# Splitting the first weight load of a decode block: 4,096 columns by themselves, as 112 plain rows and 8 groups of 2 rows

## The chip, the cores and the metric

The kernel runs on one core of a Trainium2 chip. The metric is the device time of one execution in microseconds. The time before is 374.37 us, the median of three runs (374.28 to 374.49). A profile is one execution recorded by the hardware profiler; its times count from the start of its span.

## The reference

One step of decoding for a batch of two, in float32: a layer norm, grouped-query attention over a cache of 4,096 positions, and a bilinear gated branch that scales the attention's output.

```python
def _A_ref(x, k_cache, v_cache, wq, wo):          # Hq 16, Hkv 8, Sk 4096, Dh 256, D 448
    q = (x @ wq).reshape(B, Sq, Hq, Dh) ...
    k = jnp.repeat(k_cache, rep, axis=1)
    v = jnp.repeat(v_cache, rep, axis=1)
    scores = jnp.einsum("bhqd,bhkd->bhqk", q, k) * (Dh ** -0.5)
    p = _softmax(scores, axis=-1)
    o = jnp.einsum("bhqk,bhkd->bhqd", p, v)
    ...  @ wo
def _B_ref(x, w_gate, w_up, w_down):              # F 1792
    ...
    return jnp.einsum("bsf,fd->bsd", g * u, w_down)

xn = _layernorm(x, axis=-1)
s = _A_ref(xn, A_k_cache, A_v_cache, A_wq, A_wo)
g = _silu(_B_ref(xn, B_w_gate, B_w_up, B_w_down))
return x + s * g
```

The caches are 2 x 8 x 4096 x 256 numbers each, 134 MB together; with the weights some 158 MB have to come into the core.

## The kernel before

Everything is brought into on-chip memory (128 partitions) by large loads, each with 128 rows, one to a partition. SP issues them all, in one queue and in the order of a list, `todo`. The list is filled by `plan(names, place, src, cuts)` and emptied by `issue(n)`, which starts the next `n` entries. An entry names what it brings, the buffer it goes to, its source in main memory, and the columns at which it is cut into several loads.

The order is: `wq0`, the first half of the query weights (28,672 bytes a row); `wg wu`, gate and up; `wd wq1`, down and the second half of the query weights; `k0`; then for each of 14 pairs of head and batch one load of 8.4 MB with its values and the next one's keys (`vk`); `wo` stands after the second of these; at the end the last keys and values, `last0` and `last1`, cut into seven loads. The two buffers of `ring` (128 x 16,384 numbers) take them in turn; `slot` holds `wd wq1` and later `wo`. The first four entries are issued at once, a later one when TensorE has read what was in its buffer. `wq0` goes to the first 7,168 columns of `ring.bufs[1]`, and `k0` lies behind it in the same buffer.

The computing engines follow the loads. `query(h)` multiplies the normed x with `wq0` or `wq1`: `rows` does 12 matmuls over blocks 0 to 11 of 512 columns and 2 over blocks 12 and 13. `ffn_in` and `ffn_out` make the gate. Then for each pair: `scores` from the keys, `softmax`, `values`; for each pair of pairs `combine`. The last two pairs have steps of their own, and `project` and `project_last` multiply with the output weights, of which the last part, `wo2`, comes in the last three loads.

`Flow` records every operation with the regions that it reads and writes and sets the semaphore waits from them. A load has a semaphore of its own count; an operation that reads what two loads brought waits for both. In the profile every recorded operation has the line of the helper that recorded it (L220), so the tiles' names tell them apart: `ring`, `slot` are the buffers, and `ring<-wq` is the load of `wq0`. TensorE's instructions for the middle pairs stand in a hardware loop.

On the host, `folded` lays the 448 rows of a weight matrix out as 128 rows of 14 blocks, and numpy arrays of that form are the kernel's inputs.

Of the kernel before, what the change touches and what calls it, by code (L numbers as in the profile page):

```python
# [22 lines left out]
EPS = 1e-5  # L23
WQ = 14 * 512
LEAD = 48

class Flow:
# [115 lines left out]
    def issue(self):  # L144
        nc = self.nc
        lead = nc.alloc_semaphore("lead")
        for _ in range(LEAD):
            nc.vector.sem_inc(lead)
# [72 lines left out]
        return add  # L221

def gated_decode_block(nc, x, first, vk, last0, last1, wq0, wdq, wo, wgu, out):
    flow = Flow(nc)
    PE, DVE, ACT, POOL, SP = [getattr(flow, e) for e in ("PE", "DVE", "ACT", "POOL", "SP")]
    names = iter(range(1000))
# [32 lines left out]
    loaded = {}  # L260
    todo = []

    def issue(n=1):
        for names, place, src, cuts in todo[:n]:
            t = place()
            width = ROW if not names[0].startswith("w") else src.shape[1] // len(names)
            for i, name in enumerate(names):
                loaded[name] = t[:, i * width:(i + 1) * width]
            if names == ["wd", "wq1"]:
                loaded["wd"], loaded["wq1"] = t[:, :14 * D], t[:, 14 * D:]  # L270
            for lo, hi in zip(cuts, cuts[1:]):
                SP.dma_start(t[:, lo:hi], src[:, lo:hi])
        del todo[:n]
# [15 lines left out]
    plan(f"k{LAST + 1} v{LAST}", ring, last0, [0, ROW, 2 * ROW])  # L289
    plan(f"v{LAST + 1} wo2", ring, last1, [0, 6144, ROW, *(ROW + i * D for i in (5, 7, 8))])  # L290
    issue(4)

# [230 lines left out]
    for first in range(0, LAST, B):  # L524
        flow.turn = first
        issue(2)
        if first == 0:
            flow.turn = None
            issue()
            flow.turn = first  # L530
        for i in range(first, first + B):
            p = softmax(i, s)
            o = bank("o")
            values(i, p, o)
            DVE.tensor_copy(ob[:, i % B], o)
            q = copy()
            POOL.tensor_copy(q, query_of(i + 1))
            s = scores(i + 1, q, two())
        total(add_head)
        cb = combine(ob)  # L540
        t = work["h"]()[:, :B * 64]
        DVE.tensor_tensor(t.rearrange("p (s k) -> p s k", s=B), cb.rearrange("p (s k) -> p s k", s=B),
                          over[:, :, None].to_broadcast([128, B, 64]), op=OP.mult)
        turn(oT, first // B, t)
# [19 lines left out]
    t = work["h"]()  # L564
# [62 lines left out]
```

## Time and profile before

| | |
|---|---|
| median of 3 runs | 374.37 us (374.28 to 374.49) |
| profiled execution, its own time | 374.3 us |
| its span, first to last instruction | 372.7 us |
| granted TensorE clock, mean | 0.766 |
| TensorE busy | 188.0 us, 50% |
| VectorE busy | 75.5 us, 20% |
| read from main memory | 158.54 MB |
| mean rate over the span | 426 GB/s |

Busy time of an engine is what its instructions took; the sixteen DMA engines are shown together, as a mean share of the sixteen. A view of short stretches ("busy time by stage") gives for each stretch the engines' busy time with the number of instructions, the granted clock, the DMA engines' share and the rate. A small packet of a queue is a load's completion mark. A wait in square brackets, [1.29 <-DMA ring<-wq], says how long the engine stood idle before the instruction and what ended it.

### The profile page before, as it was taken

To read this page: it belongs to the slowest core of one execution; us is meant where nothing else is said; L and a number is where in the kernel's file an instruction comes from. 1 tells how busy PE (TensorE), PEld (TensorE's weight loads), DVE (VectorE), ACT (ScalarE), POOL (GpSimd) and SP (SyncE) were. 2 spreads that over 40 slices of the span, in tenths; PEclk is the share of its full clock that TensorE was granted. 3 is DMA by queue.
4 is the path that set the end of the run, shared out by engine and by line. 5 is a ranking of instruction groups with operands and counts; after the bars stand their busy time and mean duration, and the time that the engine had idled before them with its cause. 6 is when DMAs were issued, how large, how long until landed. Compare 5 with 4: busy or idle time off the path is not lost. (4 is left out here: it accounts for less than half of the span.)

```text
span 372.7 us, 3346 instructions
## 1 busy us (share of the span) xinstructions
PE 188.0 (50%) x1474; PEld 57.2 (15%) x1474; DVE 75.5 (20%) x124; ACT 26.7 (7%) x44; POOL 5.6 (2%) x28
## 2 busy tenths in 40 slices
PE   0818292171900626555453638271919090908786
PEld 0201020020200201111121102020202030202223
DVE  2101013021130030313031212221131304030430
ACT  1101011001010010101000000101010101010121
POOL 0100000000000000000000000000000000000000
PEclk9968598596875685958595958695867586776999
DMA  8999999999999999999999999999999999999995
GB/s 339 466 424 410 429 433 450 443 445 396 425 459 436 450 443 436 429 394 450 436 450 443 436 429 394 450 436 450 443 436 429 394 450 436 450 397 443 421 414 233
DMA packets 3897, 158.67 MB, mean 426 GB/s; under 512 B 562, under 2 KB 692, under 8 KB 820
## 3 DMA queue, kind: packets, MB, share of 16 engines
q1 hardware_dynamic: 3888, 158.59, 98.6%
q8 instruction: 4, 0.07, 0.1%
q14 instruction: 1, 0.01, 0.0%
q10 hardware_dynamic: 4, 0.00, 0.0%
HBM read 158.54 MB, written 0.06 MB: 426 GB/s over the span
## 5 line engine op out<-in xcount | busy, mean ns | idle before, releaser
L220 PE MATMUL o<-ring,pT 128*32 128x512 f32 x480 | 81.4, 840 | 115.3 <-PEq L172 115.3
L220 PE MATMUL s<-ring,qc 128*32 128x512 f32 x448 | 50.7, 592 | 0.0
L220 PEld LDWEIGHTS o<-ring,pT 128*32 128x32 f32 x480 | 20.7, 149 | 163.5 <-issue 163.5
L220 DVE COPY ob<-o 128x512 f32<-128x512 f32 x14 | 9.7, 692 | 155.9 <-PE o L220 155.9
L220 ACT ACTIVATE p<-s,m 128x1024 f32<-128x1024 f32 x16 | 17.8, 1113 | 287.5 <-DVE m L220 287.5
L220 DVE TENSOR_REDUCE m<-s 128x1 f32<-128x1024 f32 x16 | 19.3, 1205 | 21.9 <-PE s L220 21.9
L220 DVE STREAM_TRANSPOSE pT<-p 128x1024 f32<-128x1024 f32 x15 | 18.7, 1245 | 19.1 <-ACT p L220 19.1
L220 PEld LDWEIGHTS s<-ring,qc 128*32 128x32 f32 x448 | 15.1, 110 | 33.0 <-issue 33.0
L220 PE MATMUL sm<-ident,m 128*1 128x128 f32 x16 | 4.3, 269 | 25.6 <-PEq L172 23.7
L220 PE MATMUL s<-ring,xnT 128*32 128x448 f32 (+1 forms) x72 | 12.1, 828 | 8.3 <-DMA ring<-wgu 8.3
L220 DVE TENSOR_REDUCE mx<-sm 1x128 f32<-1x512 f32 x16 | 10.9, 679 | 8.0 <-PE sm L220 8.0
L220 PE MATMUL sm<-one,mx 1*128 1x1 f32 x16 | 3.2, 198 | 12.9 <-PEq L172 12.1
L220 PE MATMUL s<-slot,hT 128*32 128x448 f32 x28 | 5.4, 885 | 8.0 <-DMA slot<-wdq 8.0
L220 POOL COPY qc<-qT 128x64 f32<-128x64 f32 x14 | 3.2, 236 | 290.9 <-PE s L220 283.6
L220 PE MATMUL s<-ring,qT 128*32 128x512 f32 x64 | 7.5, 597 | 0.0
L220 PEld LDWEIGHTS sm<-ident,m 128*1 128x1 f32 x16 | 1.3, 79 | 35.1 <-issue 32.9
L220 DVE RECIPROCAL over<-sm 128x2 f32<-128x2 f32 x8 | 1.4, 170 | 23.9 <-PE sm L220 23.9
L220 PE MATMUL s<-ident,pT 2*128 2x2 f32 x4 | 0.6, 247 | 10.5 <-DVE pT L220 10.5
L220 PE MATMUL cb<-ob,add_blocks 128*32 128x128 f32 x128 | 5.2, 279 | 0.6 <-ACT ob L220 0.6
L220 PEld LDWEIGHTS s<-ring,xnT 128*32 128x32 f32 x72 | 2.6, 145 | 17.0 <-DMA ring<-wgu 9.2
L220 PE MATMUL s<-ring,oT 128*32 128x112 f32 (+2 forms) x76 | 5.1, 314 | 0.1
L220 PE MATMUL wide<-slot,oT 128*32 128x448 f32 x48 | 4.9, 539 | 0.0
(65 smaller groups left out, 60.9 us busy)
## 6 DMA issues: line engine op xcount, KB each, us to landing
ring<-last SPq DMA_DIRECT2D x2, 4096.0 KB, 26.3
slot<-wdq SPq DMA_DIRECT2D x1, 6720.0 KB, 42.2
ring<-wgu SPq DMA_DIRECT2D x1, 6272.0 KB, 26.0
slot<-wo SPq DMA_DIRECT2D x1, 5376.0 KB, 46.6
ring<-first SPq DMA_DIRECT2D x1, 4096.0 KB, 51.2
ring<-wq SPq DMA_DIRECT2D x1, 3584.0 KB, 11.7
ring<-last SPq DMA_DIRECT2D x1, 3072.0 KB, 21.1
ring<-last SPq DMA_DIRECT2D x1, 1120.0 KB, 23.7
```

The source lines that it names most:

```text
L220: self.flow.record(self.engine, lambda: method(out, *args, **kw), writes, reads, name == "dma_start")
```

## The change

The first 4,096 of the 7,168 columns of `wq0` come as two loads ahead of the rest. The host cuts `wq0` into three arrays: `wqs`, the first 112 rows of these columns; `wqx`, the other 16 rows, as 8 groups of 2 rows with a third, empty row behind each group; and `wq0`, the remaining 3,072 columns of all 128 rows. `issue` starts three loads in place of one: `wqs` to partitions 0 to 111; the two filled rows of each group to partitions 112 to 127; and the rest to columns 4,096 to 7,167. The empty rows are not read. They keep the groups apart in main memory, so that the built source has the dimensions 8 (a step of 12,288 numbers), 2 (a step of 4,096) and 4,096, and the target 16 and 4,096. Every byte ends up where it was before.

```diff
+SHARE = 8
+EACH = 2
+COLS = 4096
...
-def gated_decode_block(nc, x, first, vk, last0, last1, wq0, wdq, wo, wgu, out):
+def gated_decode_block(nc, x, first, vk, last0, last1, wq0, wqs, wqx, wdq, wo, wgu, out):
...
         for names, place, src, cuts in todo[:n]:
             t = place()
             width = ROW if not names[0].startswith("w") else src.shape[1] // len(names)
+            if names == ["wq0"]:
+                most = 128 - SHARE * EACH
+                loaded["wq0"] = t[:, :WQ]
+                SP.dma_start(t[:most, :COLS], wqs)
+                SP.dma_start(t[most:, :COLS], wqx[:, :EACH])
+                SP.dma_start(t[:, COLS:WQ], src)
+                continue
...
     wq0, wq1 = [folded(wq[:, h], 512) for h in range(2)]
+    most = 128 - SHARE * EACH
+    wqs = c(wq0[:most, :COLS])
+    wqx = np.zeros((SHARE, EACH + 1, COLS), np.float32)
+    wqx[:, :EACH] = wq0[most:, :COLS].reshape(SHARE, EACH, COLS)
+    wq0 = c(wq0[:, COLS:])
```

On SP's queue, at the start of the program, the loads before are these; the name behind the arrow is the source's, without its numbers, so `wq` is `wq0` and `last` either of `last0` and `last1`.

```order
L220 DMA ring<-wq 128x7168
L220 DMA ring<-wgu 128x12544
L220 DMA slot<-wdq 128x13440
L220 DMA ring<-first 128x8192
L220 DMA ring<-vk 128x16384 x2
```

And after, at the same place:

```order
L223 DMA ring<-wqs 112x4096
L223 DMA ring<-wqx 16x1x4096
L223 DMA ring<-wq 128x3072
L223 DMA ring<-wgu 128x12544
L223 DMA slot<-wdq 128x13440
L223 DMA ring<-first 128x8192
L223 DMA ring<-vk 128x16384 x2
```

One load has become three, and those behind it have moved back by two places. On TensorE, the first query before, with its waits on the semaphores (`s0` is that of the load):

```order
4 L220 MATMUL s<-ring,xnT 32x512 [waits s7,s0]
5 L220 MATMUL s<-ring,xnT 32x512
6 L220 MATMUL s<-ring,xnT 32x512 [waits s7]
7 L220 MATMUL s<-ring,xnT 32x512 x9
8 L220 MATMUL s<-ring,oT 64x512 x2
```

And after, where `s0`, `s1` and `s2` are those of the three loads:

```order
4 L223 MATMUL s<-ring,xnT 32x512 [waits s9,s1,s0]
5 L223 MATMUL s<-ring,xnT 32x512
6 L223 MATMUL s<-ring,xnT 32x512 [waits s9]
7 L223 MATMUL s<-ring,xnT 32x512 x5
8 L223 MATMUL s<-ring,xnT 32x512 [waits s2]
9 L223 MATMUL s<-ring,xnT 32x512 x3
10 L223 MATMUL s<-ring,oT 64x512 x2
```

The first matmul waits for two loads in place of one, and the ninth, which reads the first block behind column 4,096, for the third. The other engines' instructions stand as they stood.

More of the change, by code (lines that the diff above doesn't have):

```diff
@@ L619 @@
     nc = bacc.Bacc("TRN2", target_bir_lowering=False, num_devices=1, dynamic_dma_scratch_size=1024)
-    arrays = dict(x=x, first=first, vk=vk, last0=last[0], last1=last[1], wq0=wq0, wdq=wdq, wo=wo, wgu=wgu)
+    arrays = dict(x=x, first=first, vk=vk, last0=last[0], last1=last[1], wq0=wq0, wqs=wqs, wqx=wqx, wdq=wdq, wo=wo, wgu=wgu)
     args = [nc.dram_tensor(n, a.shape, mybir.dt.from_np(a.dtype), kind="ExternalInput").ap()
```

## Prediction

> **What bounds the kernel now.** I read the page first, then the chain of work that ended last, then the busy time of short stretches at the end of the load stream.
>
> ```profile
> span 372.7 us, 3346 instructions
> PE 188.0 (50%) x1474; PEld 57.2 (15%) x1474; DVE 75.5 (20%) x124; ACT 26.7 (7%) x44; POOL 5.6 (2%) x28
> ...
> DMA  8999999999999999999999999999999999999995
> ...
> DMA packets 3897, 158.67 MB, mean 426 GB/s; under 512 B 562, under 2 KB 692, under 8 KB 820
> ...
> q1 hardware_dynamic: 3888, 158.59, 98.6%
> q8 instruction: 4, 0.07, 0.1%
> q14 instruction: 1, 0.01, 0.0%
> q10 hardware_dynamic: 4, 0.00, 0.0%
> ```
>
> No compute engine is busy for more than half of the span, while the sixteen DMA engines are full in every slice but the first and last. Queue q1 (SP's loads and the store) fills 98.6% of them. Its packets also show how a load is split: 27 DMAs of 128 rows at 128 data packets and 16 small completion packets make 27 x 144 = 3888. So each of them runs on 16 engines, 8 rows to an engine. q10 holds the two one-row loads of x: 4 packets, one row and one completion each. The engine count follows the shape.
>
> The chain that ended last, start and length in us:
>
> ```profile
> 344.56 23.68 DMA ring<-last
> ...
> 368.28 2.14 PE s L220 x64
> ...
> 370.44 0.29 DVE gate L220
> ...
> 370.75 0.27 DVE gate L220
> ```
>
> The end is a load plus a fixed 4.4 us of matmuls, two vector operations and the store. What counts is when the slowest DMA engine delivers its last row. The next rows are stretches of the span; the last three columns are TensorE's clock, the share of the sixteen DMA engines in use, and GB/s. A packet counts where it starts.
>
> ```profile
> 0.00:1.50 1.50, 0.00 (x0) 0.00 (x0) 0.00 (x0) 0.00 (x0) 0.78 (x8) 1.00 0.00 0
> 1.50:2.00 0.50, 0.00 (x0) 0.00 (x0) 0.00 (x0) 0.48 (x1) 0.00 (x0) 1.00 3.00 749
> ...
> 167.00:206.00 39.00, 20.18 (x162) 6.32 (x158) 8.65 (x13) 2.41 (x4) 0.47 (x2) 0.73 1.00 434
> ...
> 367.80:368.00 0.20, 0.20 (x16) 0.14 (x8) 0.00 (x0) 0.00 (x0) 0.00 (x0) 1.00 0.90 350
> 368.00:368.20 0.20, 0.20 (x8) 0.00 (x0) 0.00 (x0) 0.00 (x0) 0.00 (x0) 1.00 0.61 224
> 368.20:368.40 0.20, 0.13 (x7) 0.12 (x9) 0.12 (x1) 0.00 (x0) 0.00 (x0) 1.00 0.41 161
> 368.40:368.60 0.20, 0.20 (x14) 0.20 (x15) 0.19 (x1) 0.00 (x0) 0.00 (x0) 1.00 0.38 152
> 368.60:368.80 0.20, 0.20 (x19) 0.20 (x15) 0.00 (x0) 0.00 (x0) 0.00 (x0) 1.00 0.31 125
> 368.80:369.00 0.20, 0.20 (x20) 0.20 (x15) 0.00 (x0) 0.00 (x0) 0.00 (x0) 1.00 0.26 99
> 369.00:369.20 0.20, 0.20 (x20) 0.20 (x10) 0.00 (x0) 0.00 (x0) 0.00 (x0) 1.00 0.23 90
> 369.20:369.40 0.20, 0.20 (x12) 0.00 (x0) 0.00 (x0) 0.00 (x0) 0.00 (x0) 1.00 0.23 90
> 369.40:369.60 0.20, 0.20 (x12) 0.17 (x12) 0.00 (x0) 0.00 (x0) 0.00 (x0) 1.00 0.10 36
> ```
>
> Mid-kernel the share is 1.00 at 434 GB/s, so one engine moves 434 / 16 = 27.1 GB/s. At the end the engines do not stop together. More than half of them run dry between 368.0 and 368.4; in 369.2 to 369.4 the share is 0.23, some four engines, and these stop near 369.5. All sixteen had the same bytes, so these four lost time earlier. Five instruction packets (q8 and q14) also ran on the DMA engines and are a likely reason, but no row says which engines they hit.
>
> Adding the nine shares gives 0.2 x 3.43 = 0.69 us of all sixteen engines after 367.8. Shared evenly, the work would end at 368.5 instead of 369.5. So no redistribution of rows can bring more than 1.0 us, or 0.27%. A measurement of this kernel can tell about 0.2%, 0.75 us.
>
> **The change, part by part.** *The tilt.* The first load, 128 rows of 28,672 bytes, becomes three. In the first, 112 rows of 16,384 bytes split evenly into 7 per engine. In the second the source's outer dimension is 8 and the target's 16; between the 1 engine of a one-row load and the 16 of a 128-row load I take 8 engines with 2 rows each, since 8 is the largest number that divides both. The third gives every engine 8 rows of 12,288 bytes. So eight engines carry one row of 16,384 bytes more than before and eight one less. At 27.1 GB/s that is 0.60 us later and 0.60 us earlier, a swing of 1.2 us which lasts, because a full stream has no gap in which a late engine could catch up.
>
> [...]
>
> If the four are in the relieved eight, they end at 368.9. The loaded eight, mostly done by 368.0 to 368.2, end at 368.6 to 368.8, still before them. Gain: 0.60 us. If engines that stop between 368.4 and 369.0 are in the loaded eight, the gain shrinks towards zero.
>
> *Two more DMAs in the stream.* The last waits of TensorE's weight loads price one:
>
> ```profile
> 368.28 0.92 PEld L220 LDWEIGHTS s<-ring,oT 128*32 128x32 f32 x40 [0.34 <-DMA ring<-last]
> ...
> 369.43 0.35 PEld L220 LDWEIGHTS s<-ring,oT 128*32 128x32 f32 x16 [0.23 <-DMA ring<-last]
> ...
> 369.97 0.16 PEld L220 LDWEIGHTS s<-ring,oT 128*32 128x32 f32 x8 [0.19 <-DMA ring<-last]
> ```
>
> Each is released by one of the last three loads. From the first to the second 1.15 us pass, for 8 x 3,584 bytes per engine (1.06 us at 27.1 GB/s); from the second to the third 0.54 us, for half of that (0.53). So a further DMA costs 0.01 to 0.09 us. I take 0.05, and 0.10 for two. Shorter rows are in this price, since 3,584 bytes is shorter than any row of the change.
>
> *SP's issues.* Two more stand ahead of the next loads.
>
> ```profile
> 0.74 0.38 SPq L220 DMA_DIRECT2D ring<-wq  x1
> 1.17 0.42 SPq L220 DMA_DIRECT2D ring<-wgu  x1
> 1.64 0.42 SPq L220 DMA_DIRECT2D slot<-wdq  x1
> 2.11 0.68 SPq L220 DMA_DIRECT2D ring<-first  x1
> ```
>
> One issue takes 0.38 to 0.68 us, so wgu, wdq and first move about 1 us back. The engines start at 1.5 to 2.0, and 7 rows of 16,384 bytes keep them busy for 4.2 us, to about 6. The second load is issued near 1.2 and the third near 1.6. A three-dimensional source has no row here; even at 4 us for that issue the engines would not run dry. Cost: nothing, hidden by the first load.
>
> Later loads do not notice either:
>
> ```profile
> ring<-wq SPq DMA_DIRECT2D x1, 3584.0 KB, 11.7
> ...
> ring<-vk SPq DMA_DIRECT2D x14, 30.0
> ```
>
> A vk load lands 30.0 us after its issue, while its 8.39 MB take 19.3 us at 434 GB/s. It waits some 10 us behind another load; a shift of 1 to 4 us per engine does not empty the queue.
>
> *TensorE's waits.* The first query waits for two loads and, at its ninth matmul, for the third.
>
> ```profile
> 12.71 0.20 PEld L220 LDWEIGHTS s<-ring,xnT 128*32 128x32 f32 x8 [1.29 <-DMA ring<-wq]
> ...
> 17.82 1.08 PE L220 MATMUL s<-ring,oT 128*64 128x512 f32 x4
> ...
> 27.22 0.20 PEld L220 LDWEIGHTS s<-ring,xnT 128*32 128x32 f32 x8 [9.21 <-DMA ring<-wgu]
> ```
>
> It starts at 12.7, ends at 18.9 and then idles to 27.2. Up to 8.3 us of delay, and the extra wait instructions, disappear in that gap. If it were used up, ffn_in would be late next.
>
> The sum: -0.60 + 0.10 = -0.50 us. The profiled execution took 374.3 us, 1.6 outside its span of 372.7; it would take 373.8. The median of the runs, 374.37, is 0.07 above it: 373.9.
>
> **The rivals.** *A, the forecast, 373.9 (373.6 to 374.4):* the tilt works at the engines' rate and relieves the late ones. For it: only four engines are late, and the loaded ones have 1.3 us of room.
>
> *B, the tilt loads a late engine, 375.1:* one of the four among the eight is enough; the end moves by +0.60 + 0.10 = +0.70 us, just at the bound. Against it: the four may share a cause and lie together. Nothing in the rows excludes it.
>
> *C, rows of few partitions collide, 375.5 (374.5 to 377.3):* the second load writes 16 partitions only, from eight engines at once, while the relieved engines go on to the third load. Every load of before writes all 128 partitions, so its 27.1 GB/s may belong to an engine or to the 8 partitions it fills. If to the engine, the 262 KB take 1.21 us; if to partitions, 2 x 27.1 GB/s move them in 4.84 us. The loaded engines lose between 0 and 3.63 us more; halfway, 1.8. Ending at 368.7 + 1.8 + 0.1 = 370.6 instead of 369.5, the kernel takes 375.5; at the far end 377.3. It decides once the extra exceeds 0.7 us, and is slower by more than 0.2% from 1.45 us on. For it: nothing downstream lets them catch up. [...]
>
> [...] No run here shows a load of few partitions yet.
>
> *D, nothing is tilted, 374.5:* if an engine is picked by the partition it fills, every engine keeps its bytes and only the 0.10 us of the two DMAs are left. The one-row loads neither support nor exclude this.
>
> **How the numbers follow.** Chances: A 0.36, C 0.34, B 0.16, D 0.14. A is likeliest by little: a tilt of this size fits the spread, but where the late engines lie is open. Faster by over 0.2% (under 373.62) takes a gain of 0.75 us, more than the 0.60 of the tilt, so only a third of A: 0.12. Slower (over 375.12): most of C (0.31) and half of B (0.08), 0.39. The rest is 0.49. The range goes from A's low end, 373.6, to 377.0, which leaves out some 0.1 on each side. A alone would span 373.6 to 374.4.
>
> **What would show it.** The packets: 3897 grows by 152 to 4049 if the second load uses eight engines (16 + 8 packets), by 160 to 4057 if sixteen. For A the shares at the end fall together, within about 1 us of the last instead of 1.5, and the last wait for ring<-last moves 0.5 us forward. For B the tail gets longer with few engines in it. For C about eight engines stop late together, so the share stays near 0.5 for 1 us or more, and the first query's ninth matmul, which waits for the third load, starts later than 13.3. D leaves the tail as it is. What makes A wrong is a late engine among the eight, or a price of the 16 partitions above 0.7 us.

## The result, and the profile after

The changed kernel takes 379.34 us (379.0 to 380.7, five runs) beside 374.37 before (374.28 to 374.62, five runs): a ratio of 1.0138, with a 95% interval of 1.0121 to 1.0154. It is 5.0 us slower. The forecast was 373.9, at most 377.0. One execution among all that follow, of the extra load of 112 rows, took 431.46 us in a slow state and is left out below.

The page of the changed kernel, the lines that answer to those of before:

```profile
span 377.6 us, 3348 instructions
...
DMA  8999999999999999999999999999999999999995
...
DMA packets 4050, 158.67 MB, mean 420 GB/s; under 512 B 587, under 2 KB 717, under 8 KB 845
...
q1 hardware_dynamic: 4040, 158.59, 98.5%
q8 instruction: 4, 0.07, 0.1%
q10 hardware_dynamic: 4, 0.00, 0.0%
q14 instruction: 2, 0.01, 0.0%
```

The share of busy DMA engines reads as before: 8, 9 ... 9, 5. That row hides the loss, since a packet counts as busy time for as long as it takes: from 4 to 6 us the share below is 1.05 at 270 GB/s, beside 1.07 at 460 before, and a packet of 16,384 bytes takes 0.98 us here (the median), beside 0.61 in the run with one load of 128 rows. The bytes are the same and the mean rate has dropped from 426 to 420 GB/s. Queue q1 has 4040 packets, 152 more than the 3888 of before. That is the count forecast for 16 completion packets of the first load and 8 of the second, so the second load did run on eight engines.

Where the rate was lost is seen in stretches of 2 us at the start. Before (the last three columns are clock, DMA share, GB/s):

```profile
4.00:6.00 2.00, 0.00 (x0) 0.00 (x0) 0.00 (x0) 0.00 (x0) 0.00 (x0) 1.00 1.07 460
6.00:8.00 2.00, 0.00 (x0) 0.00 (x0) 0.86 (x3) 0.00 (x0) 0.00 (x0) 1.00 0.93 401
8.00:10.00 2.00, 0.00 (x0) 0.00 (x0) 1.19 (x5) 0.00 (x0) 0.68 (x3) 1.00 0.90 387
10.00:12.00 2.00, 1.51 (x6) 0.93 (x6) 1.39 (x7) 0.00 (x0) 0.25 (x2) 1.00 1.32 563
12.00:14.00 2.00, 2.00 (x10) 0.40 (x12) 0.00 (x0) 0.97 (x4) 0.65 (x3) 1.00 0.93 401
```

The changed kernel in the same stretches, and in the middle of its span:

```profile
4.00:6.00 2.00, 0.00 (x0) 0.00 (x0) 0.00 (x0) 0.00 (x0) 0.00 (x0) 1.00 1.05 270
6.00:8.00 2.00, 0.00 (x0) 0.00 (x0) 0.00 (x0) 0.00 (x0) 0.00 (x0) 1.00 0.94 263
8.00:10.00 2.00, 0.00 (x0) 0.00 (x0) 1.02 (x3) 0.00 (x0) 0.00 (x0) 1.00 1.27 242
10.00:12.00 2.00, 0.00 (x0) 0.00 (x0) 1.19 (x5) 0.00 (x0) 0.84 (x3) 1.00 0.81 125
12.00:14.00 2.00, 1.67 (x6) 0.93 (x6) 1.24 (x7) 0.00 (x0) 0.24 (x2) 1.00 0.81 313
...
167.00:206.00 39.00, 19.99 (x154) 6.29 (x158) 8.66 (x13) 2.41 (x4) 0.47 (x2) 0.72 1.00 435
```

From 4 to 14 us the kernel before brought in 4.42 MB, the changed one 2.43 MB (each rate times 2 us, added up). The missing 2.0 MB are 4.6 us at 434 GB/s. This sum is rough, since a packet counts where it starts and the rows differ in size; up to 20 us it gives less. The landings are firmer. From SP's queue and the times from issue to landing, in the changed kernel:

```profile
2.08 0.49 SPq L223 DMA_DIRECT2D ring<-wq  x1
2.61 0.52 SPq L223 DMA_DIRECT2D ring<-wgu  x1
...
ring<-wgu SPq DMA_DIRECT2D x1, 6272.0 KB, 29.6
...
ring<-wq SPq DMA_DIRECT2D x1, 1536.0 KB, 15.3
```

The last part of `wq0` lands at 17.4 (2.08 + 15.3), where the whole of it landed at 12.4 before (0.74 + 11.7). Gate and up land at 32.2, before at 27.2 (1.17 + 26.0). So 5.0 us are lost by the time `wq0` is in. Later the stream runs at 435 GB/s, as before, and nothing is caught up. The first load, 112 rows, runs at some 260 GB/s with every engine "busy" (shares of 1.05 and 0.94 from 4 to 8 us); around the 16 rows, 10 to 12 us, the rate falls to 125.

At the other end, the last waits of TensorE's weight loads in the changed kernel:

```profile
373.32 1.40 PEld L223 LDWEIGHTS s<-ring,oT 128*32 128x32 f32 x56 [0.26 <-DMA ring<-last]
...
374.91 0.16 PEld L223 LDWEIGHTS s<-ring,oT 128*32 128x32 f32 x8 [0.19 <-DMA ring<-last]
```

The last one started at 369.97 before and starts at 374.91 now, 4.9 us later. Behind it nothing has changed.

### The profile page after: what moved, and what is told of

It is laid out like the page before. It is cut to its first block, busy times and chain, and to the rows that moved or that the text cites. A ratio compares the mean times of both kernels' runs of the same rounds, so it can differ in the third digit from the quotient of the medians.

```text
span 377.6 us, 3348 instructions
## 1 busy us (share of the span) xinstructions
PE 187.2 (50%) x1474; PEld 57.2 (15%) x1474; DVE 75.5 (20%) x124; ACT 26.8 (7%) x44; POOL 5.6 (1%) x28
## 3 DMA queue, kind: packets, MB, share of 16 engines
q1 hardware_dynamic: 4040, 158.59, 98.5%
## 5 line engine op out<-in xcount | busy, mean ns | idle before, releaser
L223 PE MATMUL s<-ring,xnT 128*32 128x448 f32 (+1 forms) x72 | 11.1, 768 | 12.0 <-DMA ring<-wgu 12.0
## 6 DMA issues: line engine op xcount, KB each, us to landing
ring<-wq SPq DMA_DIRECT2D x1, 1536.0 KB, 15.3
```

The lines of the kernel that those rows point to most:

```text
L223: self.flow.record(self.engine, lambda: method(out, *args, **kw), writes, reads, name == "dma_start")
```

## The experiments

Each run was timed in turns with the kernel before. The edits are cut to the lines that matter; "..." marks lines left out, and remarks behind # are added here. The theories that the expectations name: *partitions* (the 27.1 GB/s belong to the partitions that are filled, in groups of eight as rival C takes it, so engines that fill the same ones share it; the groups are the theory's, and no run shows which partitions would form such a group), *price per load or for short rows*, and *tilt on a late engine*.

**One load of 128 rows for the first columns.**

```diff
-                SP.dma_start(t[:most, :COLS], wqs)
-                SP.dma_start(t[most:, :COLS], wqx[:, :EACH])
+                SP.dma_start(t[:, :COLS], wqs)          # wqs: all 128 rows
```

> The same first 4,096 columns come by themselves, but as one plain load of all 128 rows; then the 3,072 others. Partitions (an engine that fills partitions of other engines collides with them): all loads fill 128 partitions as before, 374.4 (374.3 to 374.6). Price per load or for short rows: two added loads cost 5.0 us, so one costs about 2.5, 376.9. Tilt on a late engine: no tilt, 374.4.

374.59 us, ratio 1.0007 (0.9997 to 1.0017): no difference. In stretches:

```profile
4.00:6.00 2.00, 0.00 (x0) 0.00 (x0) 0.00 (x0) 0.00 (x0) 0.00 (x0) 1.00 0.96 410
6.00:8.00 2.00, 0.00 (x0) 0.00 (x0) 1.47 (x4) 0.00 (x0) 0.00 (x0) 1.00 1.03 438
```

These are rows of 16,384 and 12,288 bytes at the full rate, with one load more. Short rows are out, and by the interval one load more costs at most 0.6 us; two cannot make up the 5.0.

**The same parts without the groups.**

```diff
-                SP.dma_start(t[most:, :COLS], wqx[:, :EACH])
+                SP.dma_start(t[most:, :COLS], wqx)      # wqx: 16 plain rows
```

> 112 rows and 16 rows, both plain, so that the 16 rows go to 16 engines with one row each and nothing is tilted. Partitions: both parts still fill partitions across the engines' own; 377 to 379.5. Tilt on a late engine: the tilt is gone, 374.5. Price per load: as many loads as in the changed kernel, 379.3.

379.13 us, ratio 1.0127 (1.0110 to 1.0144), as slow as the change within the intervals. Here every engine has as many bytes as before. So the loss is not the tilt's: 112 and 16 rows are slow without it. The two medians differ by 0.2 us, less than the intervals can tell, so what the tilt adds in the changed kernel is not known.

**Half the columns.**

```diff
-COLS = 4096
+COLS = 2048
```

> The changed kernel with 2,048 columns in the split part instead of 4,096, the number of loads unchanged. Partitions: the cost is a rate, so it halves with the bytes, 376.9 (376.5 to 377.3). Price per load: unchanged, 379.3. Tilt: half of 0.6 us, at most 374.8.

376.38 us, ratio 1.0057 (1.0036 to 1.0078), which is 1.3 to 2.9 us against the 5.0 of the change, with the same three loads. The median, 1.9 us, lies a little below half and below the range expected. The cost grows with the bytes and is not one per load.

**Two halves of 64 rows.**

```diff
-                most = 128 - SHARE * EACH
+                most = 64
...
                 SP.dma_start(t[:most, :COLS], wqs)      # 64 plain rows
-                SP.dma_start(t[most:, :COLS], wqx[:, :EACH])
+                SP.dma_start(t[most:, :COLS], wqx)      # 64 plain rows
```

> The first 4,096 columns as two plain loads of 64 rows, partitions 0 to 63 and 64 to 127, nothing tilted and no odd row count. Partitions: if two engines share the same eight partitions, each half goes at half the rate, 1.05 MB in 4.8 us instead of 2.4, twice: up to +4.8, 379.2, and at least 376.8 if the halves overlap in part. Engine rate alone: 374.5. If an engine follows its partitions, the two halves run beside each other: 374.5.

379.50 us, ratio 1.0134 (1.0117 to 1.0151). In stretches:

```profile
4.00:6.00 2.00, 0.00 (x0) 0.00 (x0) 0.00 (x0) 0.00 (x0) 0.00 (x0) 1.00 0.97 198
6.00:8.00 2.00, 0.00 (x0) 0.00 (x0) 1.19 (x3) 0.00 (x0) 0.00 (x0) 1.00 0.96 213
8.00:10.00 2.00, 0.00 (x0) 0.00 (x0) 1.22 (x4) 0.00 (x0) 0.87 (x3) 1.00 1.12 229
```

The rate is 198 to 229 GB/s, half of 434, with no tilt, no groups and no odd number of rows, and the sum of 4.8 us for two halves comes out within 0.2.

**Two loads of 64 rows, even and odd partitions.**

```diff
-                SP.dma_start(t[:most, :COLS], wqs)
-                SP.dma_start(t[most:, :COLS], wqx[:, :EACH])
+                SP.dma_start(t[0::2, :COLS], wqs)       # the even rows
+                SP.dma_start(t[1::2, :COLS], wqx)       # the odd rows
```

> The first 4,096 columns as two plain loads of 64 rows again, but the even partitions and then the odd ones, so that each load reaches all of the core's partition groups. If only the number of groups that a load reaches counts, nothing is lost: 374.7. If it counts which engines meet at the same moment (rows dealt in blocks of four, two engines on one group, the other half of the groups idle): 379.2 as with the lower and upper halves; in between if the engines drift apart.

377.61 us, ratio 1.0084 (1.0065 to 1.0103). This looks like "in between", but it is another cost. SP's queue in this run:

```profile
0.74 0.54 SPq L221 DMA_DIRECT2D ring<-wqs  x1
5.92 0.48 SPq L221 DMA_DIRECT2D ring<-wqx  x1
```

and its waits (total, number, longest):

```profile
SPq L221 <- DMA ring<-wqs: 4.6, 1, 4.6
```

The odd rows were issued only when the even ones had landed. `Flow.region` leaves out the step: it takes 64 partitions at a step of two for 64 in a row, and so saw two writes to the same place. The even rows themselves landed within 5.92 us, where the lower half of the run with two halves took 7.6 us from issue to landing and was still under way at half rate (213 GB/s from 6 to 8 us). The run could not tell the theories apart; a repeat without the wait could.

```diff
                 box = self.region(ap)
...
+                if dma and o["dma"] and at < 12:
+                    continue
```

> Even and then odd partitions again, without the wait that the recorder had put between the two loads: it takes a strided range of partitions for a full one, and so in the run before SP waited 4.6 us for the even rows before it issued the odd ones. If a load that reaches all groups of partitions goes at the full rate, nothing is left to pay but two loads: 374.6 (374.4 to 374.8). If engines that meet on a group lose as with the lower and upper halves: 379.2, and the first load's rows land at 7.5 us or later.

374.87 us, ratio 1.0010 (1.0000 to 1.0021). In stretches:

```profile
4.00:6.00 2.00, 0.00 (x0) 0.00 (x0) 0.66 (x2) 0.00 (x0) 0.00 (x0) 1.00 1.02 418
6.00:8.00 2.00, 0.00 (x0) 0.00 (x0) 1.29 (x5) 0.00 (x0) 0.45 (x1) 1.00 1.05 449
```

These are loads of 64 rows at the full rate. The time is 0.07 us above the range expected. Half and half costs 5.0 us, even and odd 0.3, with equal row counts, row lengths and numbers of loads. Only the partitions differ. The packet records say the same of single rows of 16,384 bytes: the median row takes 0.61 us here and in the plain load of 128 rows, 1.28 in the halves and 0.98 in the changed kernel.

**All 128 rows as groups.**

```diff
-                SP.dma_start(t[:most, :COLS], wqs)
-                SP.dma_start(t[most:, :COLS], wqx[:, :EACH])
+                SP.dma_start(t[:, :COLS], wqx[:, :EACH])   # SHARE = 64
```

> The first 4,096 columns of all 128 rows as one load, read as 64 groups of 2 rows like the 8 groups of the change (an unused row behind each group); 16 engines, 8 rows each, no tilt. If the form of the read costs anything by itself, it shows here; by the partitions theory only the assignment of rows to engines counts: 374.6 if the rows are dealt as in a plain load of 128 rows, up to 379.4 if each engine takes 8 partitions in a row, because then two engines meet on the same partitions all the time.

375.00 us, ratio 1.0013 (1.0003 to 1.0022). The form of the read, groups with a gap, costs 0.5 us here (0.1 to 0.8), where it stands first in the queue; its rate was 426 GB/s from 4 to 6 us.

**The tilt by itself, on partitions where nothing collides, and where it does.** An extra load of 8 groups of 2 rows goes into columns that nothing uses.

```diff
+            if names == ["wg", "wu"]:
+                SP.dma_start(t[0:32:2, src.shape[1]:], spare[:, :2])
```

> The kernel before, with one load more behind wq0: 8 groups of 2 rows of 15,360 bytes, into columns that nothing uses, on partitions 0, 2, ... 30, so that eight engines with two rows each fill partitions that, if engine e owns four in a row, are their own. Each of the eight carries 1.13 us more and nobody less. Partitions: no collision, so only the tilt shows. If the late engines are among the other eight, the eight loaded ones have 1.3 us of room: 374.4 to 374.6. If a late one is among the eight: 375.5. This is the tilt of the prediction without its collisions.

375.58 us, ratio 1.0034 (1.0021 to 1.0046). Its page shows the eight engines again, 24 packets more than before:

```profile
DMA packets 3921, 158.91 MB, mean 425 GB/s; under 512 B 570, under 2 KB 700, under 8 KB 828
```

The end moved by 1.09 us (375.58 - 374.49), the whole of the 1.13 that the eight engines got more. With 1.3 us of room they would have hidden most of it. So at least one of the late engines should be among those eight; the 421 GB/s shown below leave no collision to explain it. This is not proven: the grouped read alone cost 0.5 us above, and the interval here begins at 0.8.

```diff
-                SP.dma_start(t[0:32:2, src.shape[1]:], spare[:, :2])
+                SP.dma_start(t[112:, src.shape[1]:], spare[:, :2])
```

> The same extra load, but on partitions 112 to 127, as in the changed kernel. Engine rate alone: the same time as with partitions 0, 2, ... 30. Partitions: eight engines squeeze into a few groups of eight partitions and disturb their owners, so 1 to 3 us more than that run, 375.5 to 377.5, and its rows take more than their 0.57 us.

378.01 us, ratio 1.0098 (1.0084 to 1.0112). The same bytes on the same number of engines cost 2.43 us more, because of the partitions alone. The difference is in the range expected, the time itself 0.5 us above it, as the run before had moved too. In stretches, with the partitions 0, 2, ... 30 and then with 112 to 127:

```profile
12.00:14.00 2.00, 2.00 (x10) 0.40 (x12) 0.20 (x2) 0.88 (x4) 0.70 (x3) 1.00 0.99 421
```

```profile
12.00:14.00 2.00, 2.00 (x10) 0.37 (x12) 0.24 (x2) 0.84 (x4) 0.70 (x3) 1.00 0.54 127
```

The 127 GB/s are near the 125 of the changed kernel. The drop covers all sixteen engines, not eight. The stretches can't show that, since a packet counts where it starts, but the packet records of the two traces can. The eight engines without extra rows go on to rows of 50,176 bytes of the next load. With partitions 0, 2, ... 30 the first of these takes 1.85 us on each of the eight; with 112 to 127 it takes 3.94 to 4.10. The extra rows themselves take 0.57 us each in the first run and up to 1.73 in the second.

**112 rows by themselves, and 128 beside them.**

```diff
+            if names == ["wg", "wu"]:
+                SP.dma_start(t[:112, src.shape[1]:], spare)
```

> The kernel before, with an extra plain load of 112 rows of 15,360 bytes into unused columns, 1.72 MB, 7 rows on each of 16 engines. Engine rate alone: 4.0 us more, 378.4. Partitions: in the changed kernel such a part took some 2.2 to 3 us beyond its bytes, so 380.5 to 381.2, later than with all 128 rows.

381.0 us, the median of three runs (380.86 to 381.44), ratio 1.0179 (1.0161 to 1.0198): 6.5 us by the medians and 6.7 by the ratio, for 1.72 MB, which are 4.0 us at 434 GB/s. The same with `t[:, ...]`, 128 rows:

> The same with 128 rows, 1.97 MB. All theories: 4.53 us of bytes and 0.05 for a load, 379.0 (378.9 to 379.2). Under the partitions theory this run, with 14% more bytes, is faster than the one with 112 rows.

379.05 us, ratio 1.0125 (1.0109 to 1.0140): 4.6 us for 1.97 MB, as its bytes ask. The stretch inside the 112 rows, and the same stretch with 128:

```profile
12.00:14.00 2.00, 2.00 (x10) 0.27 (x12) 0.31 (x3) 0.74 (x4) 0.71 (x3) 1.00 0.92 265
```

```profile
12.00:14.00 2.00, 2.00 (x10) 0.40 (x12) 0.19 (x2) 0.90 (x4) 0.70 (x3) 1.00 1.00 430
```

There are 16 rows fewer and the end comes 2.0 us later. So the 112 rows carry a price of their own, 2.5 to 2.8 us at this row length.

## Why the prediction was wrong

*The step that failed* is the first one of the tilt: "At 27.1 GB/s that is 0.60 us later and 0.60 us earlier". The 27.1 GB/s were taken as an engine's own, whatever partitions it fills. So the loads of 112 and of 16 rows entered the sum with their bytes and "0.10 for two", and what it costs to fill only some of the partitions was put at nothing. It measured 5.0 us, and 4.6 with plain rows and no tilt (379.13 beside 374.50). The rows of before could not tell this from a rate of the partitions, as rival C said, because every load there fills all 128. The halves beside even and odd partitions settle it: both on sixteen engines (4048 packets in q1, 16 completions for each load), with the same bytes, half the rate in one (198 to 229 GB/s) and the full rate in the other (418 and 449).

*Rival C named the cause that the runs show, the partitions that are filled, and missed the size.* It came out at 375.5, at most 377.3; the kernel took 379.3. Two terms were off. First, C priced the 16 rows only. The 112 rows passed as "split evenly into 7 per engine" at no cost; by the extra loads they carry 2.5 to 2.8 us for rows of 15,360 bytes (6.5 to 6.7 less 4.0), and an estimated 2.7 to 3.0 for 16,384. Second, the 16 rows: C took 1.8 us halfway and charged them to eight engines. The pair of extra loads gives 2.43 us, an estimated 2.6 at the change's row length, and shows that all sixteen slow down (rows of 3.94 to 4.10 us in place of 1.85 on the other eight). With 0.1 for two loads the sum is 5.4 to 5.7, more than the measured 5.0; the two collisions stand directly behind each other, so part of one may lie in the other. How much was not measured.

*Forecast A's condition probably did not hold either.* It needed the late engines among the relieved eight. The extra load on partitions of its own points to a late one among the loaded, which is rival B's condition, if both loads run on the same eight engines; no view shows that. Had nothing collided, B's +0.70 would have been the likelier answer and the change would not have paid. Inside the changed kernel B's 0.6 us is not seen: with plain rows and no tilt it is as slow within the intervals (379.13 and 379.34). How far the tilt and the collisions cover each other stays open.

*What held.* A full stream does not catch up: the 5.0 us lost when `wq0` is in are still missing at the end, 4.9. The price of a load, 0.05, is not contradicted: 0.07% for one more (interval -0.03 to 0.17%), 0.3 us. The second load uses eight engines, as the packets show, so D is out. The issue of the grouped read, which had no row, takes 0.82 us:

```profile
0.74 0.40 SPq L223 DMA_DIRECT2D ring<-wqs  x1
1.20 0.82 SPq L223 DMA_DIRECT2D ring<-wqx  x1
```

It stays hidden behind the first load, as assumed. And the first query's delay vanishes in its gap; its ninth matmul, whose wait is for the third load, starts at 17.4, later than the 13.3 named for C:

```profile
17.44 0.15 PEld L223 LDWEIGHTS s<-ring,xnT 128*32 128x32 f32 x4 [0.99 <-DMA ring<-wq]
```

*The tail* was forecast for C as a share near 0.5 for 1 us. In the changed kernel:

```profile
371.80:372.20 0.40, 0.26 (x12) 0.02 (x4) 0.00 (x0) 0.26 (x1) 0.00 (x0) 1.00 0.78 314
372.20:372.60 0.40, 0.00 (x0) 0.00 (x0) 0.00 (x0) 0.40 (x1) 0.00 (x0) 1.00 0.63 233
372.60:373.00 0.40, 0.32 (x12) 0.32 (x16) 0.00 (x0) 0.03 (x1) 0.00 (x0) 1.00 0.50 179
373.00:373.40 0.40, 0.40 (x16) 0.14 (x12) 0.01 (x1) 0.00 (x0) 0.00 (x0) 1.00 0.32 121
```

The share does pass 0.78, 0.63 and 0.50 over 1.2 us, a slower fall than the 0.90, 0.61, 0.41 within 0.6 us of before. But the whole tail lies 4 us later, since the relieved engines were held up as well. That was not foreseen.

*What stays open:* how the rows of a 112-row load are dealt to the engines, and so why it drops to some 260 GB/s and costs 2.5 to 2.8 us beyond its bytes; no run here shows it. No faster version came out of the runs: the plain load of 128 rows is the best form that they have.

## What to carry to other kernels

In these runs the rate of a load hung on the partitions that its rows fill: 128 rows ran at the full rate (410 and 438 GB/s), and so did every second partition (418 and 449), while half of the partitions in a row ran at half the rate (198 to 229) and 112 of them at some 60% (242 to 270). Few rows need not hurt: 16 rows on partitions 0, 2, ... 30 left the stream at 421 GB/s, 16 on neighbouring partitions brought it to 127. So before rows are moved between DMA engines to balance them, ask which partitions the moved rows fill: a small tilt that needs an uneven set of rows can cost several times what it evens out, here 5.0 us where 0.60 was hoped for. And a "busy" DMA engine need not move at its full rate, as the share of 1.05 at 270 GB/s showed: read GB/s in short stretches beside the share.

## What was not expected of the hardware

- 112 rows in a plain load move at 242 to 270 GB/s in the changed kernel and at 265 in the extra load, with DMA shares of 0.92 and more, against 430 for 128 rows.
- Eight engines that fill 16 neighbouring partitions bring the whole stream down to 125 to 127 GB/s in a stretch of 2 us (by the starts of packets), and the other eight engines' rows take 3.94 to 4.10 us in place of 1.85, while the same load on partitions 0, 2, ... 30 leaves it at 421.
- SP takes 0.82 us to issue the grouped read of 16 rows behind another load and 0.63 for the grouped read of 128 rows as the first, beside 0.38 to 0.40 for a plain first load.
